# Backward dV and dK stored, and V loaded, a whole head at a time

## The chip, the cores and the metric

One core of a Trainium2 chip runs the kernel once. The metric is the device time of one execution in microseconds (us); shorter is better. Times of single executions of the kernel before are 1365.99, 1366.36 and 1366.83 us, median 1366.36 us.

## The reference, cut to what matters

One token with 640 features goes through an adaptively normalised attention block with a cache of 32 heads (8192 positions, 192 features each) and through a small mixer and MLP; then all gradients for the inputs are computed from `grad_out`.

```python
mod = (silu(c) @ w_mod).reshape(1, 6, 1, -1)      # sa, ca, ga, sb, cb, gb
h = layernorm(x) * (1 + ca) + sa
q = (h @ wq)                                       # 32 heads x 192
p = softmax(einsum('bhqd,bhkd->bhqk', q, k_cache) * 192 ** -0.5)
o = einsum('bhqk,bhkd->bhqd', p, v_cache)
x = x + ga * (o @ wo)
h = layernorm(x) * (1 + cb) + sb
x = x + gb * B(h)                                  # w1, w2, w3, w4 and gelu
# results: out, and d/d(x, k_cache, v_cache, wq, wo, w3, w4, c, w_mod)
```

With one query, the gradient of the cache is an outer product for each head: dV = p (8192) x do (192), and dK = dS (8192) x q (192), where dS = p * (V @ do - c). So K and V are read, V a second time in the backward pass, and dK and dV are written. Each of these has 32 heads of 3072 KB in bf16 (3.146 MB).

## The kernel before, in words

The positions of a head lie on 128 partitions, 64 positions each, so one head is 24576 contiguous bytes per partition both in DRAM and in SBUF. A half (t = 0 or 1) is 32 positions, 12288 bytes per partition, 1536 KB.

**Buffers.** `k_mem` (six halves) holds K in the forward pass. In the backward pass its halves 0 to 4 receive dV and dK, and half 5 is slot 4 of V. `v_mem` (four halves) holds V: slots 0 to 3. Slot 5 is a tile of the pool `bv`.

**Backward pass.** Iteration i of 32 (the loop near the end, over `HS`) treats head h = 31 - i and prepares the next head `nxt`:
- `bwd_mult(h, t)` (L133 through `mul`, matmuls L1109): VectorE (DVE) multiplies a half of V in place by do; TensorE (PE) adds up the product. From i = 20 on this is done one iteration ahead, between `bwd_ds` and `bwd_dk`.
- `bwd_dv(nxt, t)`: dV for the next head. In each half ScalarE (ACT) makes 20 of the 32 positions (L1114) and DVE 12 (L1090); the store of the half follows (L1117).
- `bwd_ds(h)` (L1135 and one more): dS from the sums of PE.
- `bwd_dk(h, t)`: DVE makes a half of dK (L1090) and stores it (L1144).

**Order.** All these loads and stores are issued by one queue, SP's, in program order; an issue that must wait holds all that are behind it. `pin_order` fixes the order on PE, DVE and ACT to the order in the program. `big_tile` hands out the halves of `k_mem` in the order of `big_order`: `[2, 3, 4, 0, 1]` over and over, so a half is written again five halves later.

**Ring.** V halves, blocks of Wo (batches for do) and blocks of Wq and Wmod share one ring of six slots; `ring_load` issues the next load as soon as the content six places earlier has been used (`freed`).

**Side work.** `dwo`, `dw4`, `dw3` stores go along in iterations 1 to 25. The five blocks of Wq (i = 11 to 15) and of Wmod (i = 18 to 22) are multiplied in place (`job_side_mul`), summed on PE, and their gradient blocks are written from the pool `sideout` (`job_side_out`). From i = 24 (`I_SIDE`) three more halves x, y, z (pool `xt`) join the places for dV and dK, and at the very end the four V slots do too (`tail_list`).

Of the kernel before, what the change touches and what calls it, by code (L numbers as in the profile page):

```python
# [20 lines left out]
def kernel(  # L21
# [26 lines left out]
    nc = tc.nc  # L48
# [174 lines left out]

    big = ctx.enter_context(tc.tile_pool(name="big", bufs=1))
    big_order = []
    tail_tiles = {}

    def big_tile(name):
        k = big_order.pop(0)
        if isinstance(k, str):  # L230
            pool, tag = tail_tiles[k]
            if tag[0] == "v":
                return v_tile(pool, int(tag[1:]))
            return pool.tile([P, JH, DH], BF16, name=name, tag=tag)
        return big_half(k)

    k_mem = big.tile([P, 6 * JH, DH], BF16, name="k_mem")

    def big_half(k):
        return k_mem[:, k * JH : (k + 1) * JH, :]  # L240
# [100 lines left out]
    def v_tile(pool, slot):  # L341
        if slot == 4:
            return big_half(5)
        if slot < 4:
            return v_mem[:, slot * JH : (slot + 1) * JH, :]
        return pool.tile([P, JH, DH], BF16, name="V_sb", tag=f"v{slot}")

    def load_v(pool, h, t, slot, eng=None):
        tl = v_tile(pool, slot)
        (eng or nc.sync).dma_start(out=tl, in_=V_hd[h][:, t * JH : (t + 1) * JH, :])  # L350
        return tl
# [434 lines left out]
    BATCHES = [(2, 3, 4), (5, 6, 7), (8, 9, 10), (11, 12, 13), (14, 15)]  # L786
    Q_AT, M_AT = 11, 18
    SIDE_W = {"wq": A_wq, "wm": w_mod}
    ring = []
    for i in range(1, HQ):  # L790
        if i > 1:
            ring += [("v", HS[i], t) for t in range(2)]
        if i % 2 == 1 and 0 < i // 2 < len(BATCHES):
            ring.append(("w", i // 2, 0))
        for name, at in (("wq", Q_AT), ("wm", M_AT)):
            if at <= i < at + NDC:
                ring.append((name, i - at, 0))
    ring_n, freed = [0], set()
    ldq = nc.sync
    NR = 6  # L800

    def ring_slot(n):
        return (4, 5, 2, 3, 0, 1)[n % NR]

    def ring_load():
        while ring_n[0] < len(ring) and (ring_n[0] < 2 or ring_key(ring_n[0] - NR) in freed):
            n = ring_n[0]
            kind, k, t = ring[n]
            slot = ring_slot(n)
            pool = bv if slot > 3 else fv  # L810
            ring_n[0] += 1
            if kind == "v":
                V_b.setdefault(k, {})[t] = load_v(pool, k, t, slot, ldq if n >= 2 else nc.sync)
            elif kind == "w":
                load_wo(k, v_tile(pool, slot))
            else:
                load_side(kind, k, v_tile(pool, slot))

    def load_wo(k, tl):
        lo, n = PS[BATCHES[k][-1]], len(BATCHES[k])  # L820
        tl = tl.rearrange("p j d -> p (j d)")[:, 0 : 3 * n * D].rearrange("p (c r) -> p c r", r=D)
        wo_b[k] = tl
        nc.sync.dma_start(out=tl.rearrange("p (b c) r -> p b (c r)", c=3), in_=A_wo[3 * lo * P : 3 * (lo + n) * P, :].rearrange("(b p c) r -> p b (c r)", p=P, c=3))

    def ring_key(n):
        return ring[n] if n >= 0 else (("v", HS[0], 0), ("v", HS[0], 1), ("v", HS[1], 0), ("v", HS[1], 1))[n]

    ring_load()
    big_order[:] = [0, 4, 1, 4, 1, 2, 3, 4, 1, 2, 3, 4, 0, 1] + [2, 3, 4, 0, 1] * HQ
    st2 = nc.sync  # L830

    do_pb = {}
# [263 lines left out]
    def vec_of(d, h):  # L1096
        return d[h // 2][:, (h % 2) * DH : (h % 2 + 1) * DH]
# [18 lines left out]
    def bwd_dv_store(o, h, t, r0, r1):  # L1116
        st2.dma_start(out=dV_hd[h][:, t * JH + r0 : t * JH + r1, :], in_=o[:, r0:r1, :])  # L1117

    def bwd_dv_dve(o, h, t, na=NAV // 2, ends=(JH,)):
        j0 = t * JH  # L1120
        r0 = 0
        for r1 in ends:
            ra = max(r0, na)
            pairs_outer(o[:, ra:r1, :], bst[h]["P2h"][:, j0 + ra : j0 + r1, :], vec_of(do_pb, h), r1 - ra)
            bwd_dv_store(o, h, t, r0, r1)
            r0 = r1

    def bwd_dv(h, t):
        o = big_tile("dV")
        bwd_dv_act(o, h, t)  # L1130
        bwd_dv_dve(o, h, t)

    def bwd_ds(h):
        dP = bsm.tile([P, J], FP32, name="dP")
# [3 lines left out]
        bst[h]["dS2"] = dS2  # L1138

    def bwd_dk(h, t):  # L1140
        o = big_tile("dK")
        j0 = t * JH
        pairs_outer(o, bst[h]["dS2"][:, j0 : j0 + JH, :], vec_of(q_pb, h), JH)
        st2.dma_start(out=dK_hd[h][:, j0 : j0 + JH, :], in_=o)  # L1144

    def job_mid():
        h2 = ccol(NDC, "h2")
# [33 lines left out]
    side_cm = []  # L1181
    I_SIDE = 24

    def tail_list(seven):
        n = 4 * (HQ - 1 - I_SIDE) - 2
        order = []
        cyc = list(seven)
        for c in range(n):
            if c == n - 10:
                cyc += ["v0", "v1"]  # L1190
                cyc = cyc[-2:] + cyc[:-2]
            if c == n - 6:
                cyc += ["v2", "v3"]
                cyc = cyc[-2:] + cyc[:-2]
            k = cyc.pop(0)
            order.append(k)
            cyc.append(k)
        return order

    dha_c = ccol(NDC, "dha_c")  # L1200
    dsc_c = ccol(NDC, "dsc_c")

# [9 lines left out]
        bcast_cols(col_bf, lo, n, side["bc"][:, lo * P : (lo + n) * P], act_copy)  # L1212

    def job_side_mul(name, u):
        w = side.pop((name, u))
        n = w.shape[1]
        mul(w, w, side["bc"][:, 0:n])
        m = 512 if n % 512 == 0 else 480
        ps = bank("b", name="js_ps")[:, 0:m]
        for k in range(n // m):  # L1220
            nc.tensor.matmul(ps, lhsT=ident_bf, rhs=w[:, k * m : (k + 1) * m], start=(k == 0), stop=(k == n // m - 1))  # L1221
        side["ps"] = ps
        freed.add((name, u, 0))

    def job_side_out(name, u, acc, rows_f, dram):
        nc.vector.reduce_sum(out=acc[:, u : u + 1], in_=side["ps"], axis=AX.X)
        n = dram.shape[1]
        o = side["out"].tile([P, n], BF16, name=name + "_o", tag="wout")
        nc.vector.tensor_scalar(out=o, in0=side["bc"][:, 0:n], scalar1=rows_f[:, u : u + 1], scalar2=None, op0=ALU.mult)
        st2.dma_start(out=dram[u * P : (u + 1) * P, :], in_=o)  # L1230

# [45 lines left out]
    def hook(i):  # L1277
        if i == 0:
            for u in wo_first:
                bwd_ttr(*u)  # L1280
            fin_do(PS[1], 1)
            bwd_dob(PS[1])
            cps[i] = (PS[1], 1, fin_c(PS[1], 1))
            return
        if i % 2 == 1:
            b = (i - 1) // 2
            bwd_wo_mult(b)
            if b > 0:
                freed.add(("w", b, 0))
                ring_load()  # L1290
        if i in fins:
            b = fins[i]
            lo, n = PS[BATCHES[b][-1]], len(BATCHES[b])
            bwd_wo_red(b)
            fin_do_rows(lo, n)
            if i % 2 == 0:
                bwd_dob(HS[i + 2] // 2)
            cps[i] = (lo, n, fin_c(lo, n))
            dq[i] = (lo, n, fin_dq_mm(lo, n))
        if i == 3:  # L1300
            dq[i] = (PS[1], 2, fin_dq_mm(PS[1], 2))
# [8 lines left out]
    o0 = tw.tile([P, JH, DH], BF16, name="dV", tag="w3T_t")  # L1310
    bwd_dv_dve(o0, HS[0], 0, 0, (8, 16, JH))
    h2_mm()
    bwd_dv_dve(big_tile("dV"), HS[0], 1, 0, (JQ, JH))
    bwd_pf(HS[1])
    o1 = big_tile("dV")
    bwd_dv_act(o1, HS[1], 0, 0, JQ)
    q_pb[PS[0]] = pair_bc(bsm, q_bf, PS[0], "q_pb", bank("s", 2, "t_ps", SB[0]))
    bwd_dv_store(o1, HS[1], 0, 0, JQ)
# [19 lines left out]
    for i in range(HQ):  # L1338
# [5 lines left out]
        if i <= AHEAD:  # L1344
            if i in SPLIT:
                bwd_pf(nxt)
            for t in range(2):
                bwd_mult(h, t, 2 if i == 0 else 1)
                if i == t == 0:
                    ring_load()  # L1350
                    c_first = fin_c(PS[0], 1)
                if i in SPLIT:
                    bwd_dv(nxt, t)
        if i not in EARLY:
            ring_load()
        if i - 1 in dq:
            fin_dq(*dq.pop(i - 1))
        if i == 0:
# [4 lines left out]
            for t in range(0 if i > 0 else 1, 2):  # L1363
                bwd_dv(nxt, t)
        if i in EARLY:
            ring_load()
        if i == 0:
            bwd_ds(h)
            dq_last(h)
# [21 lines left out]
        if i == NPH - 1:  # L1391
            fin_dq(*dq.pop(i))
            mm_cm.__exit__(None, None, None)
            psum_cm.__exit__(None, None, None)
            psum[0] = ctx.enter_context(tc.tile_pool(name="psum_s", bufs=1, space=bass.MemoryType.PSUM, reuse_waits="tile"))
            SB[0] = 1024
            for nm, b in (("out", 2), ("bcp", 1)):
                side_cm.append(tc.tile_pool(name="side" + nm, bufs=b, side="right", reuse_waits="tile"))
                side[nm] = side_cm[-1].__enter__()
        for f in J2[i]:  # L1400
            f()
        if i == I_SIDE:
            while side_cm:
                side_cm.pop().__exit__(None, None, None)
            xt = ctx.enter_context(tc.tile_pool(name="xt", bufs=1, side="right", reuse_waits="tile"))
            for k in "xyz":
                tail_tiles[k] = (xt, "xt" + k)
            for n in range(len(ring) - NR, len(ring)):
                slot = ring_slot(n)
                tail_tiles[f"v{n - len(ring) + NR}"] = (bv if slot > 3 else fv, f"v{slot}")  # L1410
            big_order[:] = tail_list(big_order[0:5] + ["x", "y", "z"])
    pin_order(first_ins)


# [28 lines left out]
```

## Time and profile before

| what | before |
|---|---|
| median of three runs | 1366.36 us |
| the profiled execution | 1367.3 us |
| its span, first to last instruction | 1365.5 us |
| moved by DMA queue q1 (the loads and stores above) | 565.86 MB |
| busy share: DVE, ACT, PE | 79%, 67%, 65% |

How to read the views: the page cuts the span into 40 slices and gives a busy digit for each engine and for the 16 DMA engines. A table by stretches gives the busy time of each engine, the granted TensorE clock, the DMA share (the time of all packets over 16 engines' time; packets that overlap on one engine count twice, so it can pass 1) and GB/s. The DMA view of a stretch counts the packets, says how many were under 512 bytes, under 2 KB and under 8 KB, and gives packets, MB and share of each queue; q8 and q14 fetch instructions. The groups of instructions give count, then busy time and mean ns of one, then the idle time of the engine just before them and what ended it. "us to landing" of a DMA counts from its issue to its completion.

### The profile page before, as it was taken

To read this page: it belongs to the slowest core of one execution; us is meant where nothing else is said; L and a number is where in the kernel's file an instruction comes from. 1 tells how busy PE (TensorE), PEld (TensorE's weight loads), DVE (VectorE), ACT (ScalarE), POOL (GpSimd) and SP (SyncE) were. 2 spreads that over 40 slices of the span, in tenths; PEclk is the share of its full clock that TensorE was granted. 3 is DMA by queue.
4 is the path that set the end of the run, shared out by engine and by line. 5 is a ranking of instruction groups with operands and counts; after the bars stand their busy time and mean duration, and the time that the engine had idled before them with its cause. 6 is when DMAs were issued, how large, how long until landed. Compare 5 with 4: busy or idle time off the path is not lost.

```text
span 1365.5 us, 27762 instructions
## 1 busy us (share of the span) xinstructions
PE 886.4 (65%) x11404; PEld 630.7 (46%) x11404; DVE 1080.0 (79%) x1220; ACT 919.9 (67%) x2564; POOL 3.2 (0%) x10
## 2 busy tenths in 40 slices
PE   3799999999999999747756764533334444224440
PEld 3577777777777777736645642211111111011110
DVE  3487888888888887799987778967768778669991
ACT  1387787877888876876776669545567654647770
POOL 0000000000000000000000000000000000000000
PEclk9999999999999999576676666676656766656675
DMA  9999999999999999699999999999999999999997
GB/s 392 417 422 428 425 420 421 420 422 420 424 415 418 424 422 405 259 399 424 423 420 425 427 426 428 424 425 427 426 425 428 426 426 429 424 427 430 427 431 327
DMA packets 55883, 567.64 MB, mean 416 GB/s; under 512 B 5708, under 2 KB 8012, under 8 KB 20172
## 3 DMA queue, kind: packets, MB, share of 16 engines
q1 hardware_dynamic: 55726, 565.86, 98.8%
q8 instruction: 89, 1.46, 0.4%
q14 instruction: 38, 0.31, 0.1%
q10 hardware_dynamic: 30, 0.00, 0.0%
HBM read 339.94 MB, written 225.91 MB: 414 GB/s over the span
## 4 chain that ended last, share of the span: by engine, by line
DMA 49%; PE 22%; DVE 18%; ACT 5%; SPq 2%; issue 2%; DVEq 0%; ACTq 0%
DMA out_dram<-k_mem 29%; DMA v_mem<-in_A_v_cache_dram 17%; PE ps_a L462 7%; DVE k_mem L1090 7%; PE ps_b L473 4%; ACT k_mem L1114 3%; DVE v_mem L133 3%; DMA k_mem<-in_A_k_cache_dram 3%; PE S_ps L402 2%; PE dP_ps L1109 2%; PE kb_ps L479 2%; DVE k_mem L133 1%; SPq L248 1%; DVE prod L133 1%; DVE dP L1135 1%
## 5 line engine op out<-in xcount | busy, mean ns | idle before, releaser
L1114 ACT ACTIVATE k_mem<-do_pb,PF 128x192 bf16<-128x192 bf16 x1126 | 394.2, 440 | 165.1 <-DMA out_dram<-k_mem 164.7
L437 ACT ACTIVATE EK<-k_mem,E_f 128x192 bf16<-128x192 bf16 x992 | 354.5, 442 | 35.8 <-issue 17.7
L1109 PEld LDWEIGHTS <-ident_bf 128*128 128x128 bf16 x1056 | 120.7, 120 | 328.8 <-DVE v_mem L133 114.0
L1109 PE MATMUL dP_ps<-v_mem,ident_bf 128*128 128x512 bf16 (+2 forms) x744 | 168.1, 400 | 139.3 <-DVE v_mem L133 139.3
L133 DVE TENSOR_TENSOR prod<-k_mem,q_pb 128x6144 bf16<-128x6144 bf16 x62 | 207.6, 3349 | 5.2 <-DMA k_mem<-in_A_k_cache_dram 3.9
L1090 DVE TENSOR_TENSOR k_mem<-dS,q_pb 128x6144 bf16<-128x6144 bf16 x59 | 195.9, 3354 | 10.7 <-DMA out_dram<-k_mem 10.1
L462 PE MATMUL ps_a<-EK,v_mem 128*128 128x193 bf16 x1984 | 192.3, 249 | 13.8 <-DMA v_mem<-in_A_v_cache_dram 13.8
L462 PEld LDWEIGHTS <-v_mem 128*128 128x128 bf16 x1984 | 164.3, 98 | 32.2 <-DMA v_mem<-in_A_v_cache_dram 17.3
L1090 DVE TENSOR_TENSOR k_mem<-P2h,do_pb 128x2304 bf16<-128x2304 bf16 (+2 forms) x58 | 78.5, 1360 | 101.4 <-DMA out_dram<-k_mem 100.4
L133 DVE TENSOR_TENSOR v_mem<-v_mem,do_pb 128x6144 bf16<-128x6144 bf16 (+1 forms) x47 | 149.7, 3214 | 0.0
L444 DVE TENSOR_TENSOR EK<-k_mem,P2h 128x1536 bf16<-128x1536 bf16 x124 | 117.8, 950 | 0.2 <-issue 0.2
L473 PE MATMUL ps_b<-EK,v_mem 128*64 128x193 bf16 x1984 | 107.8, 251 | 0.0
L402 PE MATMUL S_ps<-prod,ident_bf 64*64 64x256 bf16 x2976 | 95.8, 275 | 6.4 <-DVE prod L133 6.3
L402 PEld LDWEIGHTS <-ident_bf 64*64 64x64 bf16 x3072 | 85.4, 110 | 26.1 <-issue 23.5
L473 PEld LDWEIGHTS <-v_mem 128*64 128x64 bf16 x1984 | 80.7, 109 | 19.3 <-issue 15.6
L1109 PE MATMUL dP_ps<-k_mem,ident_bf 128*128 128x256 bf16 (+1 forms) x168 | 39.2, 404 | 47.1 <-DVE k_mem L133 47.1
L479 PE MATMUL kb_ps<-EK,hot_bf 128*32 128x384 bf16 x992 | 63.6, 333 | 0.0
L1221 PEld LDWEIGHTS <-ident_bf 128*128 128x128 bf16 x100 | 13.0, 130 | 104.8 <-issue 101.9
L1109 PE MATMUL dP_ps<-V_sb,ident_bf 128*128 128x256 bf16 (+1 forms) x144 | 34.0, 405 | 26.8 <-DVE V_sb L133 26.8
L442 DVE CAST EK<-E_f 128x16 bf16<-128x16 f32 x124 | 24.4, 196 | 32.5 <-ACT EK L437 21.7
L423 ACT ACTIVATE E_f<-sm_ps,negm 128x64 f32<-128x64 f32 x31 | 9.7, 314 | 58.9 <-DVE negm L421 58.9
L406 DVE TENSOR_REDUCE S<-S_ps 128x128 f32<-128x1024 f32 x32 | 39.2, 1224 | 10.8 <-PE S_ps L402 10.7
(289 smaller groups left out, 931.9 us busy)
## 6 DMA issues: line engine op xcount, KB each, us to landing
out_dram<-k_mem SPq DMA_DIRECT2D x114, 1536.0 KB, 23.6
v_mem<-in_A_v_cache_dram SPq DMA_DIRECT2D x55, 1536.0 KB, 21.6
v_mem<-in_A_v_cache_dram SPq DMA_DIRECT2D x25, 3072.0 KB, 17.8
k_mem<-in_A_k_cache_dram SPq DMA_DIRECT2D x20, 3072.0 KB, 14.2
k_mem<-in_A_k_cache_dram SPq DMA_DIRECT2D x24, 1536.0 KB, 19.2
k_mem<-in_A_v_cache_dram SPq DMA_DIRECT2D x10, 1536.0 KB, 20.7
V_sb<-in_A_v_cache_dram SPq DMA_DIRECT2D x9, 1536.0 KB, 23.1
wq<-in_A_wq_dram SPq DMA_DIRECT2D x3, 2560.0 KB, 33.9
```

Source lines behind the costliest of these rows:

```text
L133: nc.vector.tensor_tensor(out=out, in0=a, in1=b, op=ALU.mult)
L402: nc.tensor.matmul(st["S_ps"][c0 : c0 + 64, r, t * JH : (t + 1) * JH, :], lhsT=ident_bf[64 * r : 64 * r + 64, 64 * r : 64 * r + 64], rhs=p ...
L406: nc.vector.reduce_sum(out=st["S2"], in_=st["S_ps"], axis=AX.X)
L437: nc.scalar.activation(out=st["EK"][q][:, jj, 0:DH], in_=K_st[h, t][:, r * JQ + jj, :], func=ACT.Copy, scale=st["E_f"][:, j : j + 1])
L442: nc.vector.tensor_copy(out=EK[:, :, DH : DH + 1], in_=st["E_f"][:, q * JQ : (q + 1) * JQ, None])
L444: nc.vector.tensor_tensor(out=EK[:, NA:JQ, 0:DH].rearrange("p j (d r) -> p j d r", r=2), in0=K_st[h, t][:, r * JQ + NA : (r + 1) * JQ, :]. ...
L462: nc.tensor.matmul(st["A_ps"][:, 0:n], lhsT=V_sb[:, r * JQ + jj, a0:a1], rhs=EK[:, jj, 0:n], start=(q == 0 and jj == 0), stop=(q == 3 and ...
L473: nc.tensor.matmul(st["B_ps"][g : g + 64, 0:n], lhsT=V_sb[:, r * JQ + jj, b0:b1], rhs=EK[:, jj, 0:n], start=(q == 0 and jj < 2), stop=(q = ...
L479: nc.tensor.matmul(kb_ps[g : g + 32, 0 : 2 * DH], lhsT=hot_bf[:, HQ - 1 - h : 2 * HQ - 1 - h], rhs=EK[:, jj : jj + 2, 0:DH], start=(h == 0 ...
L1090: nc.vector.tensor_tensor(out=o.rearrange("p j (d r) -> p j d r", r=2), in0=pairs[:, :, None, :].to_broadcast([P, n, NP2, 2]), in1=vec.rea ...
L1109: nc.tensor.matmul(bst[h]["dP_ps"][:, t * JH + r : t * JH + r + n, :], lhsT=ident_bf, rhs=V_sb[:, :, k * w : (k + 1) * w], start=(k == 0), ...
L1114: nc.scalar.activation(out=o[:, jj, :], in_=vec_of(do_pb, h), func=ACT.Copy, scale=bst[h]["PF"][:, t * JH + jj : t * JH + jj + 1])
```

## The change

Heads are counted here by their place in the backward pass, 0 (h = 31) to 31 (h = 0).

- dV of the heads 9 to 31 and dK of the heads 8 to 30 go to whole places A, B, C of `k_mem` (halves 0-1, 2-3, 4-5), in the order B, C, A. Both halves are computed as before, and one DMA stores the head after the second half. From dV of head 26 on (iteration 25) a fourth place X joins; the last dV and the last dK but one use the two halves of `v_mem` (V1, V0), and the last dK is stored as two halves from (0, 1). Earlier heads use pairs of halves and are stored by halves, in the order of before.
- V of the heads 10 to 31 is loaded by one DMA into one of two whole slots of `v_mem`, issued as soon as both halves of the head two before have been used. Until then there are five V slots (0 to 4).
- Wo blocks, each in turn, go to slot 5 alone. Wq and Wmod blocks use slot 5 and two new tiles of a pool `sidew`; the gradient block is written into the tile of its own block and stored from it, and the block three later is loaded into that tile two iterations after (`W_AT`). The pool `sideout` and the tiles x, y, z are gone.

```diff
-    ring = []
-    for i in range(1, HQ):
-        if i > 1:
-            ring += [("v", HS[i], t) for t in range(2)]
...
+    V_SLOTS = [(2, 3), (0, 1), (4, 2), (3, 0), (1, 4), (2, 3), (0, 1)]
+    v_jobs = [(3 + k, t, sl[t], 1) for k, sl in enumerate(V_SLOTS) for t in range(2)]
+    v_jobs += [(k, 0, 2 * (k % 2 == 0), 2) for k in range(3 + len(V_SLOTS), HQ)]
+    v_occ = dict(enumerate([(1, 0), (1, 1), (0, 0), (0, 1), (2, 0)]))
+    W_USE = [("wq", u, Q_AT + u) for u in range(NDC)] + [("wm", u, M_AT + u) for u in range(NDC)]
+    W_AT = {}
+    for n, (name, u, use) in enumerate(W_USE):
+        W_AT.setdefault(10 + (n > 1) if n < 3 else W_USE[n - 3][2] + 2, []).append(n)
...
+    def ring_load(i):
+        if i == 2:
+            load_wo(1, v_tile(bv, 5))
+        while v_jobs and all(("v", HS[v_occ[sl][0]], v_occ[sl][1]) in freed for sl in range(v_jobs[0][2], v_jobs[0][2] + v_jobs[0][3])):
+            k, t, slot, n = v_jobs.pop(0)
+            for r in range(n):
+                v_occ[slot + r] = (k, t + r)
+            if n == 1:
+                V_b.setdefault(HS[k], {})[t] = load_v(fv, HS[k], t, slot)
             else:
-                load_side(kind, k, v_tile(pool, slot))
+                V_b[HS[k]] = {r: v_tile(fv, slot + r) for r in range(2)}
+                nc.sync.dma_start(out=v_pair(k), in_=V_hd[HS[k]])
+        for n in W_AT.get(i, ()):
+            name, u, use = W_USE[n]
+            load_side(name, u, v_tile(bv, 5) if n % 3 == 0 else side["w"].tile([P, JH, DH], BF16, name="W_sb", tag=f"sw{n % 3}"))
+
+    def out_place(k):
+        if isinstance(k, tuple):
+            return [big_half(x) for x in k], None
+        tl = places[k]
+        return [tl[:, 0:JH, :], tl[:, JH : 2 * JH, :]], tl
+
+    for n, k in enumerate("ABC"):
+        places[k] = k_mem[:, 2 * n * JH : 2 * (n + 1) * JH, :]
...
-    big_order[:] = [0, 4, 1, 4, 1, 2, 3, 4, 1, 2, 3, 4, 0, 1] + [2, 3, 4, 0, 1] * HQ
+    V_b[HS[2]] = {0: load_v(bv, HS[2], 0, 4), 1: load_v(bv, HS[2], 1, 5)}
+    big_order[:] = [0, 4]
+    outs = [(1, 2), (3, 4), (1, 2), (3, 4), (0, 1), (2, 3), (4, 0), (1, 2), (3, 4), (0, 1), (2, 3), (4, 0), (1, 2), (3, 4), (0, 1)]
+    outs += list("BCA") * 11 + ["B"]
+    outs += ["X", "C", "A", "B"] * 2 + ["X", "C", "V1", "V0", (0, 1)]
...
     def bwd_dv(h, t):
-        o = big_tile("dV")
-        bwd_dv_act(o, h, t)
-        bwd_dv_dve(o, h, t)
+        if "dv" not in bst[h]:
+            bst[h]["dv"] = out_place(outs.pop(0))
+        halves, whole = bst[h]["dv"]
+        bwd_dv_act(halves[t], h, t)
+        bwd_dv_dve(halves[t], h, t, store=whole is None)
+        if whole is not None and t == 1:
+            st2.dma_start(out=dV_hd[h], in_=whole)
...
     def bwd_dk(h, t):
-        o = big_tile("dK")
+        if t == 0:
+            bst[h]["dk"] = out_place(outs.pop(0))
+        halves, whole = bst[h]["dk"]
         j0 = t * JH
-        pairs_outer(o, bst[h]["dS2"][:, j0 : j0 + JH, :], vec_of(q_pb, h), JH)
-        st2.dma_start(out=dK_hd[h][:, j0 : j0 + JH, :], in_=o)
+        pairs_outer(halves[t], bst[h]["dS2"][:, j0 : j0 + JH, :], vec_of(q_pb, h), JH)
+        if whole is None:
+            st2.dma_start(out=dK_hd[h][:, j0 : j0 + JH, :], in_=halves[t])
+        elif t == 1:
+            st2.dma_start(out=dK_hd[h], in_=whole)
...
     def job_side_out(name, u, acc, rows_f, dram):
...
-        o = side["out"].tile([P, n], BF16, name=name + "_o", tag="wout")
+        o = side.pop((name, u))
...
-            for nm, b in (("out", 2), ("bcp", 1)):
+            for nm, b in (("w", 1), ("bcp", 1)):
...
+            places["X"] = xt.tile([P, 2 * JH, DH], BF16, name="xt")
+            for k in range(2):
+                places[f"V{k}"] = v_mem[:, 2 * k * JH : 2 * (k + 1) * JH, :]
```

More of the change, by code (lines that the diff above doesn't have):

```diff
@@ L225 @@
     big_order = []
-    tail_tiles = {}
+    places = {}
     def big_tile(name):
[L229 to L235, printed above, removed]
+        return big_half(big_order.pop(0))
     k_mem = big.tile([P, 6 * JH, DH], BF16, name="k_mem")
@@ L788 @@
     SIDE_W = {"wq": A_wq, "wm": w_mod}
-    ring = []
-    for i in range(1, HQ):
-        if i > 1:
-            ring += [("v", HS[i], t) for t in range(2)]
[L793 to L815, printed above, removed]
-            else:
-                load_side(kind, k, v_tile(pool, slot))
+    freed = set()
@@ new lines, with v_pair @@
+    w_half = {}
+    def v_pair(k):
+        return v_mem[:, 2 * (k % 2 == 0) * JH : 2 * (k % 2 == 0) * JH + 2 * JH, :]
+    def ring_load(i):
[7 more added lines that the diff above has]
+                V_b.setdefault(HS[k], {})[t] = load_v(fv, HS[k], t, slot)
+            else:
+                V_b[HS[k]] = {r: v_tile(fv, slot + r) for r in range(2)}
[3 more added lines that the diff above has]
+            load_side(name, u, v_tile(bv, 5) if n % 3 == 0 else side["w"].tile([P, JH, DH], BF16, name="W_sb", tag=f"sw{n % 3}"))
@@ L823, in load_wo @@
         nc.sync.dma_start(out=tl.rearrange("p (b c) r -> p b (c r)", c=3), in_=A_wo[3 * lo * P : 3 * (lo + n) * P, :].rearrange("(b p c) r -> p b (c r)", p=P, c=3))
-    def ring_key(n):
-        return ring[n] if n >= 0 else (("v", HS[0], 0), ("v", HS[0], 1), ("v", HS[1], 0), ("v", HS[1], 1))[n]
-    ring_load()
-    big_order[:] = [0, 4, 1, 4, 1, 2, 3, 4, 1, 2, 3, 4, 0, 1] + [2, 3, 4, 0, 1] * HQ
+    V_b[HS[2]] = {0: load_v(bv, HS[2], 0, 4), 1: load_v(bv, HS[2], 1, 5)}
[3 more added lines that the diff above has]
+    outs += ["X", "C", "A", "B"] * 2 + ["X", "C", "V1", "V0", (0, 1)]
     st2 = nc.sync
@@ L1117, in bwd_dv_store, with bwd_dv_dve @@
         st2.dma_start(out=dV_hd[h][:, t * JH + r0 : t * JH + r1, :], in_=o[:, r0:r1, :])
-    def bwd_dv_dve(o, h, t, na=NAV // 2, ends=(JH,)):
+    def bwd_dv_dve(o, h, t, na=NAV // 2, ends=(JH,), store=True):
         j0 = t * JH
@@ L1124, in bwd_dv_dve @@
             pairs_outer(o[:, ra:r1, :], bst[h]["P2h"][:, j0 + ra : j0 + r1, :], vec_of(do_pb, h), r1 - ra)
-            bwd_dv_store(o, h, t, r0, r1)
+            if store:
+                bwd_dv_store(o, h, t, r0, r1)
             r0 = r1
     def bwd_dv(h, t):
-        o = big_tile("dV")
-        bwd_dv_act(o, h, t)
-        bwd_dv_dve(o, h, t)
+        if "dv" not in bst[h]:
[5 more added lines that the diff above has]
+            st2.dma_start(out=dV_hd[h], in_=whole)
     def bwd_ds(h):
@@ L1182 @@
     I_SIDE = 24
[L1184 to L1198, printed above, removed]
     dha_c = ccol(NDC, "dha_c")
@@ L1214, in job_side_mul @@
     def job_side_mul(name, u):
-        w = side.pop((name, u))
+        w = side[name, u]
         n = w.shape[1]
@@ L1222, in job_side_mul @@
         side["ps"] = ps
-        freed.add((name, u, 0))
     def job_side_out(name, u, acc, rows_f, dram):
@@ L1287, in hook @@
             bwd_wo_mult(b)
-            if b > 0:
-                freed.add(("w", b, 0))
-                ring_load()
+            if 0 < b < len(BATCHES) - 1:
+                load_wo(b + 1, v_tile(bv, 5))
         if i in fins:
@@ L1312 @@
     h2_mm()
-    bwd_dv_dve(big_tile("dV"), HS[0], 1, 0, (JQ, JH))
+    bwd_dv_dve(big_half(big_order.pop(0)), HS[0], 1, 0, (JQ, JH))
     bwd_pf(HS[1])
-    o1 = big_tile("dV")
+    bst[HS[1]]["dv"] = out_place((1, 4))
+    o1 = bst[HS[1]]["dv"][0][0]
     bwd_dv_act(o1, HS[1], 0, 0, JQ)
@@ L1349 @@
                 if i == t == 0:
-                    ring_load()
+                    ring_load(0)
                     c_first = fin_c(PS[0], 1)
@@ L1354 @@
         if i not in EARLY:
-            ring_load()
+            ring_load(i)
         if i - 1 in dq:
@@ L1365 @@
         if i in EARLY:
-            ring_load()
+            ring_load(i)
         if i == 0:
@@ L1405 @@
             xt = ctx.enter_context(tc.tile_pool(name="xt", bufs=1, side="right", reuse_waits="tile"))
[L1406 to L1411, printed above, removed]
+            places["X"] = xt.tile([P, 2 * JH, DH], BF16, name="xt")
+            for k in range(2):
+                places[f"V{k}"] = v_mem[:, 2 * k * JH : 2 * (k + 1) * JH, :]
     pin_order(first_ins)
```

## The prediction

> **What bounds the kernel now.** I read the page's slices first, then the table by stretches, then the DMA view of single stretches.
>
> ```profile
> span 1365.5 us, 27762 instructions
> ...
> DMA  9999999999999999699999999999999999999997
> ...
> q1 hardware_dynamic: 55726, 565.86, 98.8%
> ```
>
> ```profile
> 100.00:480.00 380.00, 364.68 (x6729) 288.92 (x6729) 317.58 (x490) 303.66 (x887) 0.00 (x0) 1.00 1.00 422
> 640.00:860.00 220.00, 138.29 (x802) 105.78 (x801) 184.04 (x177) 154.75 (x409) 0.00 (x0) 0.66 1.01 425
> 860.00:1140.00 280.00, 114.15 (x401) 45.57 (x399) 215.74 (x128) 170.31 (x455) 0.00 (x0) 0.68 1.01 426
> 1160.00:1340.00 180.00, 63.83 (x220) 24.60 (x218) 153.76 (x87) 117.03 (x336) 0.00 (x0) 0.66 1.01 428
> 540.00:580.00 40.00, 31.69 (x493) 29.51 (x491) 31.16 (x89) 30.31 (x78) 2.09 (x2) 0.54 0.73 281
> 1340.00:1365.50 25.50, 0.00 (x0) 0.00 (x0) 0.00 (x0) 0.00 (x0) 0.00 (x0) 0.50 0.69 293
> ```
>
> The last two numbers of a row are the DMA share and GB/s. Outside the middle (540 to 580) and the last 25 us the 16 DMA engines are never short of work, and in the backward pass they move 425 to 428 GB/s. DVE is busy 154 of 180 us in the stretch from 1160, ACT 117: neither is the bound there. What they wait for says the same:
>
> ```profile
> L1114 ACT ACTIVATE k_mem<-do_pb,PF 128x192 bf16<-128x192 bf16 x1126 | 394.2, 440 | 165.1 <-DMA out_dram<-k_mem 164.7
> ...
> L1090 DVE TENSOR_TENSOR k_mem<-P2h,do_pb 128x2304 bf16<-128x2304 bf16 (+2 forms) x58 | 78.5, 1360 | 101.4 <-DMA out_dram<-k_mem 100.4
> ```
>
> ACT stood still for 165 us and DVE for 101 us until a store had left its place. Those waits are the price of a full DMA queue, not its cause. So the change can gain in two ways only: the same bytes pass the DMA engines in less time, or an empty stretch is filled. It can lose by one: the queue runs dry where it is full now. The bytes stay the same, and the two empty stretches lie outside what the change touches (the middle is before the first whole transfer, the end is the drain after the last store is issued).
>
> **The change part by part.** *Fewer and larger packets.* Whole places are handed out 34 times as B, C, A and 12 times by the last list without its pair (0, 1): 46 stores. V is loaded whole for heads 10 to 31: 22 loads. That is 68 transfers of 3072 KB for 136 of 1536 KB. Each has one packet per partition, so each engine moves 8 packets of 24576 bytes for 16 of 12288: 68 x 8 = 544 packets fewer on every engine. What is one packet worth, apart from its bytes? No row shows a store of 24576 bytes; loads of it are in the forward pass.
>
> Four stretches, by their DMA view: 40 to 60 (blocks of wq in 4096-byte packets, and halves), 60 to 80 (halves, forward), 341 to 362 (wholes, forward), 1320 to 1340 (halves, stores):
>
> ```profile
> DMA packets 1309, 8.38 MB, mean 419 GB/s; under 512 B 76, under 2 KB 76, under 8 KB 903
> ...
> q1 hardware_dynamic: 1307, 8.35, 101.5%
> q8 instruction: 2, 0.03, 0.7%
> ```
>
> ```profile
> DMA packets 769, 8.42 MB, mean 421 GB/s; under 512 B 84, under 2 KB 84, under 8 KB 84
> ...
> q1 hardware_dynamic: 764, 8.36, 99.7%
> ```
>
> ```profile
> DMA packets 415, 9.00 MB, mean 428 GB/s; under 512 B 48, under 2 KB 48, under 8 KB 48
> ...
> q1 hardware_dynamic: 412, 8.95, 99.8%
> q8 instruction: 3, 0.05, 1.0%
> ```
>
> ```profile
> DMA packets 786, 8.58 MB, mean 429 GB/s; under 512 B 88, under 2 KB 88, under 8 KB 88
> ...
> q1 hardware_dynamic: 786, 8.58, 100.6%
> ```
>
> The packets under 512 bytes are completions; I leave them in the time and out of the count. A half then takes 99.7% x 320 us / 680 = 469.2 ns in the forward pass and 100.6% x 320 / 698 = 461.2 ns in the stores; a whole takes 99.8% x 336 / 364 = 921.2 ns. In the stretch from 40 there are 827 packets of 4096 bytes and 404 halves: 324.8 us less 404 x 469.2 ns leaves 163.5 ns for 4096 bytes. Three of these carry the bytes of one half and take 490.5 ns, 21.3 more for two packets more: 10.7 ns a packet. Part of that overlaps with the next packet, since the shares pass 100%: by (324.8 + 2.2 - 320) / 1231 = 5.7 ns a packet from 40, by 1.9 us / 698 = 2.8 ns in the stores. I take the mean of the two, 4.2 ns, off: **6.5 ns a packet, 544 x 6.5 = 3.5 us**.
>
> The bounds come from the same rows. Two halves of the forward pass against a whole there: 938.4 - 921.2 = 17 ns for the packet saved, 9.2 us in all. Two halves of the stores against the forward whole: 922.4 - 921.2 = 1.2 ns, 0.7 us. The second compares a stage with instruction fetches (1.0% on q8) with one without, and the first mixes 20 us stretches of unlike neighbours; 6.5 is between, nearer to the lower end, and I keep both for the range. Below zero I see no reason: the 422 GB/s of the forward whole-head stretch (100 to 480) are less than the 425 to 428 of the halves in the backward pass, but it also carries instruction fetches (q8) and the 480 KB pieces of Wo, and the halves of the forward pass (60 to 80) run at 421.
>
> *Coarser places.* A place is now free only when a whole head has landed, and a store starts only when a whole head is made. I follow one iteration of the steady part (i = 10 to 19). The rows:
>
> ```profile
> 1147.86 1.22 DVE L1135 TENSOR_REDUCE dP<-dP_ps 128x64 f32<-128x1024 f32 x1
> ...
> 1149.39 6.62 DVE L133 TENSOR_TENSOR v_mem<-v_mem,do_pb 128x6144 bf16<-128x6144 bf16 x2
> ...
> 1182.98 6.62 DVE L1090 TENSOR_TENSOR k_mem<-dS,q_pb 128x6144 bf16<-128x6144 bf16 x2
> ...
> 1214.71 3.10 PE L1109 MATMUL dP_ps<-V_sb,ident_bf 128*128 128x512 bf16 x12
> ...
> 1222.06 13.92 ACT L1114 ACTIVATE k_mem<-do_pb,PF 128x192 bf16<-128x192 bf16 x40
> ```
>
> ```profile
> out_dram<-k_mem SPq DMA_DIRECT2D x13, 1536.0 KB, 23.2
> v_mem<-in_A_v_cache_dram SPq DMA_DIRECT2D x4, 1536.0 KB, 25.8
> ```
>
> ```profile
> out_dram<-dV SPq DMA_DIRECT2D x2, 384.0 KB, 2.4
> ```
>
> The second fence is the stretch 1200 to 1300: a half needs 3.7 us of DMA and lands 23 to 26 us after its issue, so some 20 us of work lie ahead of it. The third (560 to 620) shows a transfer with nothing ahead: 2.4 us for 0.9 us of bytes, so about 1.5 us to complete. A whole takes 3.146 MB / 429 GB/s = 7.3 us. SP issues in the order V(i+2), dV(i+1), dK(i).
> - dK(i) goes where dV(i) was. Behind dV(i) in the queue lie dK(i-1), V(i+2) and dV(i+1): 22 us. Until dK(i) is issued pass 1.5 + 6.6 us. **14 us of work remain.**
> - dV(i+1) goes where dK(i-2) was. Behind that lie V(i+1), dV(i), dK(i-1), V(i+2): 29 us; needed are 1.5 + 13.9 (ACT; the two parts of DVE beside it). 14 us remain.
> - V(i+2) needs V(i) used up: DVE makes dK(i-1) once dV(i-1) has landed, then multiplies, then PE ends: 1.5 + 6.6 + 6.6 + 3.1 = 17.8 us. Behind dV(i-1) lie dK(i-2), V(i+1), dV(i), dK(i-1): 29 us. 11 us remain.
>
> So the reserve falls from about 20 to 11 to 14 us and does not end. In front of the whole store SP can hold the load behind it, but these sums have that order already. From i = 20 the multiplication is done an iteration ahead and the reserve of V grows.
>
> *Wq and Wmod.* Same ten loads and ten stores. A block loaded in iteration U+2 waits on SP for the store of iteration U, which has a whole iteration behind it (with a block of Wq 3 x 7.3 + 2 x 3.7 = 29 us); the multiplication comes one iteration later. Nothing waits long: 0, and hidden by the reserve if it does. *Wo, first block of the ring*: it is issued in iteration 2, at the place where the row of SP below stands, and needed where DVE's row stands; a load of that stretch (620 to 700) lands after 15.1 us.
>
> ```profile
> 623.98 0.55 SPq L350 DMA_DIRECT2D k_mem<-in_A_v_cache_dram  x1
> ```
>
> ```profile
> 644.33 3.08 DVE v_mem L133
> ```
>
> ```profile
> v_mem<-in_A_v_cache_dram SPq DMA_DIRECT2D x4, 1536.0 KB, 15.1
> ```
>
> That is 5 us to spare, and a late landing would be borne by the queue: 0. *Places and sums otherwise* (X, V1, V0; six halves for five): 0, since the DMA engines are full either way.
>
> **Sum.** The profiled execution took 1367.3 us: span 1365.5 and 1.8 around it; it is 0.9 above the median. 1367.3 - 3.5 = 1363.8 for it, and 1366.36 - 3.5 = **1362.9 us** for the median of three. A measurement can tell about 0.2% from no change, 2.7 us: below 1363.6 it is faster, above 1369.1 slower.
>
> **The rivals.**
> *The packet costs less than I take.* Against my 6.5 ns stand the 1.2 ns of the stores' half and the equal GB/s of the forward stretches with halves (421) and wholes (422). At 3.5 ns the gain is 544 x 3.5 = 1.9 us: 1364.5, within 0.2%. A change that does not do what it says ends here too: were whole stores cut into halves by the DMA, V alone would gain 22 x 8 x 6.5 ns = 1.1 us: 1365.2. The Trainium skill ("DMA: Bandwidth & Descriptors", section "Why small descriptors are slow (HBM only)") speaks for this rival: besides a cycle for each 32 bytes a packet costs about three fixed cycles, so by its account 3 of 387 for a half. Of 20 us x 16 / 698 = 458.5 ns that would be 3.6 ns, an estimate, and 1364.4 us. The 10.7 ns of the small packets, even less the 4.2 of overlap, speak against it.
> *The reserve runs out.* Where side work delays DVE or ACT by more than the 11 to 14 us, the queue is dry until the whole head is made, where before a half sufficed. Up to there it costs nothing, beyond it each us late is a us lost, in up to 22 iterations. Were each of these 0.4 us short: 8.8 - 3.5 = 5.3 us slower, 1371.7. For it: DVE is busy 85% in the stretch from 1160. Against it: in the forward pass V has the same two whole slots, and the share stays at 1.00.
> *The packet costs all of 17 ns*: 1357.2.
>
> **How the numbers follow.** Forecast 0.53 (5 to 8.7 ns, 1361.6 to 1363.7), cheap packet or no whole stores 0.26, reserve 0.17, dear packet 0.04. All of the reserve's chance but 0.01 is above 1369.1; of the forecast 0.02 falls short of 1363.6. Faster 0.55, same 0.29, slower 0.16. The range leaves out the dear packet and the far half of the reserve: 1360.5 to 1371.
>
> **What would show it.** Right: in stretches of whole transfers the DMA view counts about half the packets, at 430 to 431 GB/s with a share still at 1.00 or above; wholes land after 18 to 25 us; the middle and the drain stay as they are. Wrong: 428 GB/s with full engines (the packet is cheap), or shares under 1.00 in the stretch from i = 9 on, with SP waiting for DVE or ACT ahead of whole stores (the reserve).

## The result and the profile after

The changed kernel took 1362.74 us in the median of 8 runs (1361.67 to 1363.02), the kernel before 1366.4 us (8 runs, 1365.64 to 1367.15): ratio 0.9972, 95% interval 0.9961 to 0.9983. That is 3.7 us less; 3.5 were forecast. The profiled execution took 1362.73 us with a span of 1360.9. The page of the changed kernel, its counts:

```profile
span 1360.9 us, 27631 instructions
...
DMA packets 46090, 567.63 MB, mean 417 GB/s; under 512 B 4620, under 2 KB 6924, under 8 KB 19084
...
q1 hardware_dynamic: 45934, 565.86, 98.7%
...
L1117 ACT ACTIVATE k_mem<-do_pb,PF 128x192 bf16<-128x192 bf16 x1086 | 378.7, 440 | 124.3 <-DMA out_dram<-k_mem 105.0
...
L1093 DVE TENSOR_TENSOR k_mem<-dS,q_pb 128x6144 bf16<-128x6144 bf16 x62 | 205.4, 3353 | 50.4 <-DMA out_dram<-k_mem 50.1
...
L1093 DVE TENSOR_TENSOR k_mem<-P2h,do_pb 128x2304 bf16<-128x2304 bf16 (+2 forms) x56 | 74.4, 1358 | 8.4 <-DMA out_dram<-k_mem 7.6
```

The bytes of q1 are the same to the last digit, the packets 9792 fewer: 68 x (128 packets and 16 completions), so all 68 transfers are whole and none was cut up. The compute engines still wait for stores to leave their places, ACT less (105 us, before 165), and DVE at another point: before dK 50 us, before dV 8 where it was 100.

The table by stretches of the changed kernel (last two numbers: DMA share, GB/s):

```profile
100.00:480.00 380.00, 362.53 (x6712) 287.31 (x6714) 317.07 (x487) 303.23 (x886) 0.00 (x0) 1.00 1.00 421
540.00:580.00 40.00, 31.37 (x494) 29.14 (x495) 31.35 (x90) 30.30 (x78) 2.07 (x2) 0.55 0.75 286
640.00:860.00 220.00, 139.12 (x815) 102.99 (x815) 186.77 (x179) 159.08 (x422) 0.00 (x0) 0.68 1.01 427
860.00:1140.00 280.00, 103.05 (x384) 42.13 (x386) 216.21 (x130) 171.42 (x462) 0.00 (x0) 0.68 1.01 429
1160.00:1336.00 176.00, 62.07 (x212) 23.85 (x212) 135.98 (x76) 108.86 (x314) 0.00 (x0) 0.65 1.01 431
```

The engines are as full as before, but they move 429 and 431 GB/s where it was 426 and 428. The forward pass and the middle did not change. One stretch that holds nothing but whole transfers (1300 to 1320; by their issues and landings two stores, with parts of two loads of V around them), in its DMA view:

```profile
DMA packets 397, 8.63 MB, mean 431 GB/s; under 512 B 46, under 2 KB 46, under 8 KB 46
...
q1 hardware_dynamic: 397, 8.63, 100.4%
```

By the prediction's reckoning a whole takes 100.4% x 320 us / 351 = 915.3 ns, two halves of stores 2 x 461.2 = 922.4: 7.1 ns less for one packet less. The figure is rough, since one packet more or less in the count shifts it by 2.6 ns. Another profile of the changed kernel has, in the same stretch, 47 completions among 399 packets:

```profile
q1 hardware_dynamic: 399, 8.65, 100.5%
```

That is 913.6 ns for a whole, 8.8 less than two halves.

How much a fixed stretch moves can be compared between kernels. From 860 to 1320 the kernel before moved (first fence) and the changed one (second):

```profile
q1 hardware_dynamic: 20041, 196.07, 100.8%
```

```profile
q1 hardware_dynamic: 12391, 197.35, 100.5%
```

1.28 MB more in 460 us; at 429 GB/s that is 3.0 us of the 3.7. The rest of the whole transfers lies before and behind this stretch. (The other profile of the changed kernel moved 197.32 MB here; two profiles of one kernel can differ by 0.2.)

### The profile page after: what moved, and what is told of

It reads as the page before. It is cut to its first block, busy times and chain, and to the rows that moved or that the text cites. A ratio compares the mean times of both kernels' runs of the same rounds, so it can differ in the third digit from the quotient of the medians.

```text
span 1360.9 us, 27631 instructions
## 1 busy us (share of the span) xinstructions
PE 870.3 (64%) x11401; PEld 621.5 (46%) x11404; DVE 1079.7 (79%) x1220; ACT 918.1 (67%) x2564; POOL 3.2 (0%) x10
## 4 chain that ended last, share of the span: by engine, by line
DMA 45%; PE 18%; DVE 15%; ACT 6%; issue 2%; DVEq 0%; SPq 0%; ACTq 0%
DMA out_dram<-k_mem 24%; DMA v_mem<-in_A_v_cache_dram 17%; DVE k_mem L1093 7%; PE ps_a L456 6%; ACT k_mem L1117 6%; PE ps_b L467 3%; DVE v_mem L133 2%; PE dP_ps L1112 2%; DMA W_sb<-in_w_mod_dram 2%; PE S_ps L396 2%; PE kb_ps L473 1%; DMA k_mem<-in_A_k_cache_dram 1%; DVE prod L133 1%; DVE k_mem L133 1%; PE t_ps L741 0%
## 5 line engine op out<-in xcount | busy, mean ns | idle before, releaser
L1117 ACT ACTIVATE k_mem<-do_pb,PF 128x192 bf16<-128x192 bf16 x1086 | 378.7, 440 | 124.3 <-DMA out_dram<-k_mem 105.0
L1112 PE MATMUL dP_ps<-v_mem,ident_bf 128*128 128x512 bf16 (+2 forms) x960 | 217.5, 400 | 259.6 <-DVE v_mem L133 259.6
L1093 DVE TENSOR_TENSOR k_mem<-dS,q_pb 128x6144 bf16<-128x6144 bf16 x62 | 205.4, 3353 | 50.4 <-DMA out_dram<-k_mem 50.1
L133 DVE TENSOR_TENSOR v_mem<-v_mem,do_pb 128x6144 bf16<-128x6144 bf16 (+1 forms) x62 | 199.1, 3248 | 32.9 <-DMA v_mem<-in_A_v_cache_dram 32.9
L1093 DVE TENSOR_TENSOR k_mem<-P2h,do_pb 128x2304 bf16<-128x2304 bf16 (+2 forms) x56 | 74.4, 1358 | 8.4 <-DMA out_dram<-k_mem 7.6
L196 ACT CAST do_pb<-bc_ps 128x384 bf16<-128x384 f32 x15 | 7.1, 471 | 92.7 <-PE bc_ps L192 92.7
L1117 ACT ACTIVATE xt<-do_pb,PF 128x192 bf16<-128x192 bf16 x120 | 41.8, 439 | 0.1
```

Source lines behind the costliest of these rows:

```text
L133: nc.vector.tensor_tensor(out=out, in0=a, in1=b, op=ALU.mult)
L1093: nc.vector.tensor_tensor(out=o.rearrange("p j (d r) -> p j d r", r=2), in0=pairs[:, :, None, :].to_broadcast([P, n, NP2, 2]), in1=vec.rea ...
L1112: nc.tensor.matmul(bst[h]["dP_ps"][:, t * JH + r : t * JH + r + n, :], lhsT=ident_bf, rhs=V_sb[:, :, k * w : (k + 1) * w], start=(k == 0), ...
L1117: nc.scalar.activation(out=o[:, jj, :], in_=vec_of(do_pb, h), func=ACT.Copy, scale=bst[h]["PF"][:, t * JH + jj : t * JH + jj + 1])
```

## The experiments

Two theories to begin with. *Size* (the expectations call it the packet theory): an engine pays for each packet besides its bytes, and 544 packets fewer are the gain. *Places*: the gain comes from six halves in place of five, and from tiles of their own for Wq and Wmod. A third, *transfer*, splits the first: the cost belongs to a DMA (its issue, its completions), not to its packets.

**Two and four pieces.**

```diff
-            st2.dma_start(out=dV_hd[h], in_=whole)
+            for r in range(2):            # 4 in the second run; dK and V likewise
+                w = 2 * JH // 2
+                st2.dma_start(out=dV_hd[h][:, r * w : (r + 1) * w, :], in_=whole[:, r * w : (r + 1) * w, :])
```

Two pieces. Expected: 

> The changed kernel with its places, waits and order kept, but each of the 68 whole transfers issued as two of half a head, one right behind the other, when the whole head is ready. Packet theory (each packet costs its engine about 6.4 ns besides its bytes): 544 packets per engine come back, +3.5 us on 1362.7, about 1366.2 us; stretches of these transfers at 427 to 429 GB/s again. Place theory (the gain came from six halves instead of five and from the new tiles for Wq and Wmod, not from the size): stays at 1362.7.

Measured: 1366.46 us (11 runs, 1365.57 to 1367.3), ratio 1.0 (0.9991 to 1.0008). All of the gain is gone with places, waits and order unchanged. The theory of places falls. From 860 to 1320 it moved:

```profile
q1 hardware_dynamic: 20054, 196.20, 100.8%
```

as little as the kernel before. Four pieces. Expected: 

> As the run with two pieces, but four transfers of a quarter head (6144 bytes per partition) for each of the 68. Packet theory with the same cost for every size: 3 x 544 = 1632 packets more per engine, +10.4 us: 1373.1. If the cost fell away with deeper queues or were hidden between neighbours: less than 1370. Place theory: 1362.7.

Measured: 1375.8 us (1375.02 to 1376.52), ratio 1.0068 (1.0054 to 1.0082). That is 9.3 us more than two pieces for 1088 packets more per engine, 8.6 ns each, against 3.7 / 544 = 6.8 ns for the first doubling. Its page counts 75310 packets on q1, and the same stretch moved less with engines as full as ever:

```profile
q1 hardware_dynamic: 34875, 192.95, 101.4%
```

**Packet or transfer, stores.** A place whose halves don't touch needs two packets per partition in one DMA. (The edit, cut: the halves and the stores take the same shape, and the places are handed out in the order C, A, B.)

```diff
-        places[k] = k_mem[:, 2 * n * JH : 2 * (n + 1) * JH, :]
+        places[k] = k_mem.rearrange("p (t k j) d -> p t k (j d)", t=2, k=3)[:, :, n, :]
```

Expected: 

> Places A, B, C made of halves that are not neighbours (0 and 3, 1 and 4, 2 and 5), each head still stored by one DMA: 41 stores keep their single issue and their 16 completions but have two packets of 12288 bytes per partition (V, X and the two places in V's memory as in the changed kernel). Packet theory: 41 x 8 = 328 packets more per engine, +2.1 us: 1364.8. Transfer theory (the cost belongs to a DMA's issue and completion): 1362.7. Place theory: 1362.7.

Measured: 1523.48 us, ratio 1.1145 (1.1129 to 1.116). Neither theory had that. Page and table by stretches of this run:

```profile
q1 hardware_dynamic: 51182, 565.86, 90.7%
...
L1095 DVE TENSOR_TENSOR k_mem<-dS,q_pb 128x6144 bf16<-128x6144 bf16 x62 | 205.9, 3354 | 190.9 <-DMA out_dram<-k_mem 190.5
```

```profile
860.00:1140.00 280.00, 88.00 (x315) 35.86 (x318) 166.63 (x99) 134.05 (x358) 0.00 (x0) 0.63 0.82 325
```

The packets are those planned (41 x 128 more), but the queue is dry: DVE stood 190 us before dK until a store had landed, against 50. The places interleave (0 and 3, 1 and 4, 2 and 5), so each spans bytes of the two others, and the waits came out as if they overlapped. The next run has the same packets without that (cut):

```diff
+    HB, GAP = JH * DH, 16        # 32 bytes; k_flat: k_mem with 4 * GAP more
+        lo = n * (2 * HB + GAP)
+        places[k] = k_flat[:, lo : lo + 2 * (HB + GAP)].rearrange("p (t x) -> p t x", t=2)[:, :, 0:HB]
```

(Four one-column constants share a tile to make room.) Expected: 

> As the run with places of halves that are not neighbours, but the two halves of each of A, B and C lie beside each other with 32 bytes between them, so that no place overlaps another: 41 stores keep one issue and 16 completions each and have two packets of 12288 bytes per partition. Packet theory (6.8 ns a packet, by the run with two pieces): 41 x 8 = 328 packets more per engine, +2.2 us: 1364.9. Transfer theory (the cost belongs to a DMA's issue and completions): 1362.7. And the 1523 us of the run before came from the waits between overlapping places, not from the packets: no stretch below 425 GB/s here.

Measured: 1364.44 us (11 runs, 1363.56 to 1365.58), ratio 0.9982 (0.9973 to 0.9991), with the same 51182 packets. So the 160 us were waits. The step over the changed kernel, 1.7 us, is near the spread, so both were run side by side. Expected: 

> The changed kernel once more, beside the two runs that follow on the same chip, since their differences are near the spread of a median. All theories: 1362.7, give or take 0.5.

and 

> The places with 32 bytes between their halves once more. Packet theory: 1.7 to 2.2 us above the changed kernel of this call. Transfer theory: equal to it.

Measured: the changed kernel 1362.61 us (1361.42 to 1363.6), ratio 0.997 (0.9958 to 0.9981); the gap 1364.05 (1363.42 to 1365.44), ratio 0.9983 (0.9974 to 0.9991). 1.4 us, after 1.7: 4.4 to 5.2 ns for each of 328 packets. So for stores the second packet costs, without a second transfer. One rival was not tested: the 32 bytes also shift where the halves begin in SBUF, and no run has the shift without the second packet.

**Packet or transfer, loads of V.**

```diff
-                nc.sync.dma_start(out=v_pair(k), in_=V_hd[HS[k]])
+                for r in range(2):
+                    w = 2 * JH // 2
+                    nc.sync.dma_start(out=v_pair(k)[:, r * w : (r + 1) * w, :], in_=V_hd[HS[k]][:, r * w : (r + 1) * w, :])
```

Expected: 

> The changed kernel with only the 22 loads of V in two pieces each, the 46 stores whole. Packet theory: 22 x 8 = 176 packets more per engine, +1.2 us: 1363.9. If only stores gain from the size: 1362.7; if only loads do: 1366.4.

Measured: 1364.8 us (11 runs, 1364.15 to 1366.21), ratio 0.9985 (0.9976 to 0.9994): 2.1 us for 176 packets. Again beside the changed kernel, expected: 

> V in two pieces once more. Packet theory with 6.8 ns for loads and stores alike: 1.2 us above the changed kernel of this call; if packets of loads cost more, as the first run seemed to say (11.9 ns), 2.1 us.

Measured: 1364.56 us (1363.56 to 1365.75), ratio 0.9983 (0.9974 to 0.9992): 2.0 us, 11 ns for each packet. Then one transfer with two packets per partition, by a gap of 32 bytes between the halves of V's two whole slots. Expected: 

> The changed kernel, but the two halves of each whole slot of V have 32 bytes between them: the 22 loads of V keep one issue each and have two packets of 12288 bytes per partition (176 packets more per engine), all else whole. Two pieces per load cost 2.0 us (11.4 ns a packet), more than the stores' 4.4 to 5.2 ns. If a load's packet costs that: 1364.6. If the packet costs 5 to 7 ns as elsewhere and the rest belongs to the second transfer: 1363.5 to 1363.9. If all belongs to the transfer: 1362.7.

Measured: 1362.19 us (5 runs, 1361.57 to 1362.74), ratio 0.996 (0.9947 to 0.9974). The same packets in one transfer cost nothing that can be seen. (This run is from another chip. It lies 4.3 us under the kernel before there; the changed kernel lay 4.2 under it beside the second run with two pieces.) So with V the loss comes with the second transfer, not with the second packet. From 860 to 1320 moved the two runs with two pieces (first and second fence) and the one with the gap (third):

```profile
q1 hardware_dynamic: 14974, 197.27, 100.6%
```

```profile
q1 hardware_dynamic: 14966, 197.07, 100.5%
```

```profile
q1 hardware_dynamic: 14689, 197.23, 100.7%
```

Against the changed kernel's 197.35 MB that is 0.2, 0.7 and 0.3 us, and the first two are profiles of one kernel. So most of the 2.0 us of the two pieces is not in the mean rate of this stretch. It shows at the end. The DMA view from 1350 to 1370 gives GB/s in slices of 0.5 us; the changed kernel (first) and the first run with two pieces (second):

```profile
GB/s 467 393 442 369 418 418 418 123 172 123 74 74 74 49 49 49 25 25 0 0 0 0 0 0 0 0 0 0 0 0 0 0 0 0 0 0 0 0 0 0
```

```profile
GB/s 467 393 418 467 221 221 147 172 74 74 74 123 49 25 25 25 25 25 25 25 25 25 0 0 0 16 0 0 0 16 0 0 0 0 0 0 0 0 0 0
```

The changed kernel moves its last data at 1359, this one at 1361. In its last nine slices 25 GB/s flow, about what one of 16 engines moves (430 / 16 = 27). So one engine is left with some 4 us of work when the others are done, though up to 1320 the kernels had moved nearly the same. Why that engine is late stays open.

**The forward pass by halves.**

```diff
-    K_WHOLE = range(5, 25)
+    K_WHOLE = range(0)
...
-    V_WHOLE = HQ - 4
+    V_WHOLE = 3
```

Expected: 

> The changed kernel with the 20 whole loads of K and 25 of V in the forward pass loaded by halves instead. Packet theory, if loads in the forward pass cost the same: 45 x 8 = 360 packets more per engine x 6.8 ns = +2.4 us: 1365.1. If the forward pass gains nothing from the size, as its equal GB/s with halves and wholes seemed to say: 1362.7.

Measured: 1365.59 us (11 runs, 1364.73 to 1367.36), ratio 0.9993 (0.9985 to 1.0002): 2.9 us above the changed kernel. The stretch 100 to 480, where 44 of the 45 loads lie, doesn't show it. The changed kernel (first) and this one:

```profile
q1 hardware_dynamic: 9408, 159.13, 99.4%
```

```profile
q1 hardware_dynamic: 15796, 159.16, 99.9%
```

The same megabytes in the same time: in the rate, neither the second packet nor the second transfer of these loads costs anything. The loss stands later, where the forward pass ends. The changed kernel (first) and this one from 520 to 540:

```profile
520.00:540.00 20.00, 19.57 (x394) 16.06 (x392) 15.64 (x32) 14.16 (x40) 0.00 (x0) 0.97 1.02 402
```

```profile
520.00:540.00 20.00, 18.35 (x351) 14.90 (x349) 14.52 (x26) 14.19 (x40) 0.00 (x0) 1.00 0.93 361
```

The share falls from 1.02 to 0.93: the queue runs dry for a while, and 0.8 MB less is moved, 1.9 us of the 2.9. So the 2.9 us are not a price of 360 packets. That halves leave less work ahead in the queue there is the likely reason; no run tests it.

**The reserve.** All dV in B, all dK in C:

```diff
-    outs += list("BCA") * 11 + ["B"]
+    outs += list("BC") * 17
```

Expected: 

> The changed kernel with two whole places instead of three up to the head of iteration 24: all dV in B, all dK in C. Reserve theory: dV of the next head must wait until dV of this one has landed; behind that lie only dK and V, 14.7 us, and 15.4 us pass until it is issued, so the queue is dry for 0.7 us or more in each of some 16 iterations, and the longer the later it gets its turn: 10 to 60 us slower than the changed kernel, 1373 to 1423, shares under 1.00 from iteration 9 on. If the queue doesn't need the third place: 1362.7.

Measured: 1373.92 us (1372.88 to 1376.97), ratio 1.0059 (1.0044 to 1.0075): 11.2 us slower than the changed kernel, at the low end of what was expected. Its table by stretches:

```profile
860.00:1140.00 280.00, 114.51 (x406) 45.86 (x408) 215.95 (x127) 168.87 (x455) 0.00 (x0) 0.67 1.00 421
1140.00:1320.00 180.00, 59.00 (x215) 23.23 (x215) 145.11 (x86) 116.80 (x336) 0.00 (x0) 0.65 0.99 418
```

429 and 430 GB/s have become 421 and 418, with shares of 1.00 and 0.99 where they were 1.01: the queue runs dry now and then. From 860 to 1320 this run moved

```profile
q1 hardware_dynamic: 12194, 192.91, 99.5%
```

4.4 MB less than the changed kernel, 10 us of the 11.2. This is how the rival would have looked.

**The dry spot at the end.** Just before the last dK but one is stored (1338) the changed kernel's engines are short of work:

```profile
1335.00:1339.00 4.00, 0.00 (x0) 0.00 (x0) 4.00 (x2) 0.00 (x0) 0.00 (x0) 0.80 0.74 320
...
1350.00:1355.00 5.00, 0.00 (x0) 0.00 (x0) 0.00 (x0) 0.00 (x0) 0.00 (x0) 0.50 0.79 334
```

```diff
-        return [tl[:, 0:JH, :], tl[:, JH : 2 * JH, :]], tl
+        return [tl[:, 0:JH, :], tl[:, JH : 2 * JH, :]], None if k == "V0" else tl
```

Expected: 

> The changed kernel, but the last dK but one (its place is V0) is stored by halves, the first 3.3 us earlier. In the changed kernel the DMA engines are short of work for about 1.2 us around 1335 to 1339, just ahead of that store. If that is its lateness: 1361.5, and the share stays at 1.00 there. If the engines lose that time at the end anyway (the slowest engine decides): 1362.7.

Measured: 1362.56 us (1361.29 to 1362.93), ratio 0.997 (0.9959 to 0.9982): no faster. The spot was filled:

```profile
1335.00:1339.00 4.00, 0.00 (x0) 0.00 (x0) 3.96 (x3) 0.00 (x0) 0.00 (x0) 0.73 0.95 406
...
1350.00:1355.00 5.00, 0.00 (x0) 0.00 (x0) 0.00 (x0) 0.00 (x0) 0.00 (x0) 0.50 0.49 209
1355.00:1360.50 5.50, 0.00 (x0) 0.00 (x0) 0.00 (x0) 0.00 (x0) 0.00 (x0) 0.50 0.12 51
```

What was moved earlier is missing later: the mean rate falls off from 1350 instead of 1355, and the end stays. The last 20 us of this run (1350 to 1370) in slices of 0.5 us:

```profile
GB/s 393 270 246 197 172 147 172 147 197 147 147 98 98 74 49 49 49 0 0 0 0 0 0 0 0 0 0 0 0 0 0 0 0 0 0 0 0 0 0 0
```

The rate falls in steps to that of two engines, and the last data move at 1358.5, in the changed kernel at 1359. So some engines finish up to 8 us before the last, and filling idle time of the others doesn't help it. That the last one was not dry before is concluded from this, not seen: the view gives the sum of the 16.

## Why the prediction was right, point by point

- *The DMA engines are the bound, and their empty stretches stay.* Right: shares of 1.00 to 1.01, 286 GB/s in the middle where it was 281. The dry spot at 1335 was not foreseen; filling it gained nothing.
- *544 packets fewer per engine.* Right: 9792 on q1 less the completions are 8704, 544 on each of 16.
- *6.5 ns a packet, 3.5 us.* Right as a sum: 3.7 us / 544 = 6.8 ns by the time. The step behind it was too simple. It gave stores and loads one price, paid by the packet. The runs split the 3.7 us. The stores' part is 1366.46 - 1364.56 = 1.9 us for 368 packets, 5.2 ns each; this is a difference of two runs, since none cuts the stores alone. V's part is 2.0 us for 176 packets, 11 ns each, and it is no packet's price: it comes with the second transfer and shows mostly in the last engine's end. At 6.5 ns the stores would have given 2.4 us and V 1.1. The two errors nearly cancel, and that is luck. So is some of the 6.5 itself: it was made from loads of 4096 bytes, less the mean of two overlaps.
- *The bounds, 1.2 and 17 ns.* Both were read from loads or from two unlike stages. The low one set halves of stores against a whole of the forward pass; against the stretch of whole transfers, mostly stores, the difference is 7.1 to 8.8 ns. The high one came from forward loads, where halves cost nothing in the rate from 100 to 480.
- *Coarser places, 11 to 14 us of reserve left.* The sign was right: no stretch went dry until 1335. The size was too low. The changed kernel from 1000 to 1100 (A, B, C alone) and from 1200 to 1300 (with X):

```profile
out_dram<-k_mem SPq DMA_DIRECT2D x8, 3072.0 KB, 27.4
```

```profile
out_dram<-k_mem SPq DMA_DIRECT2D x7, 3072.0 KB, 31.5
v_mem<-in_A_v_cache_dram SPq DMA_DIRECT2D x5, 3072.0 KB, 30.4
```

  A whole store lands 27 us after its issue in the steady part and 31 later; 18 to 25 had been expected. Less 7.3 us for itself and 1.5 to complete, that is 19 to 22 us of other work ahead. The sums counted V, dV and dK alone and left out the side work in the same queue; whether this is the whole difference stays open. The two-places run then came to 0.7 us x 16 = 11 us as the same sums gave at least, and 11.2 were measured. As the sums were 5 us or more too low for three places, a hit that close is in part luck; the order (three places hold, two don't) is what was shown.
- *Wq, Wmod, Wo and the places otherwise: 0.* With two pieces the time is the one before (1366.46 against 1366.63 on the same chip), so these together come to nothing measurable.
- *The rival of the cheap packet, 1.9 us.* Wrong for the whole: 3.7 us were gained. The rule of the Trainium skill ("DMA: Bandwidth & Descriptors", section "Why small descriptors are slow (HBM only)"), about three fixed cycles a packet, was 3.6 ns by the prediction's estimate; the runs show more for stores, 4.4 to 5.2 ns for the second packet. For loads the rival was nearer than the forecast: the equal GB/s of the forward stretches was good evidence, since 44 loads by halves cost nothing in the rate, and V's second packet in one transfer cost nothing either.

## What to carry to other kernels

When the DMA queue is full all the time, count packets and transfers per engine, not bytes alone: here some 5 ns for each packet of 12288 bytes that the stores saved, 1 part in 90, while loads showed no price in the rate. Before making transfers larger, follow for each place what lies in the queue between its landing and the next issue from it, since a coarser place pays only while that stays above the time to fill it. And a full queue is a matter of the slowest engine: idle time that a mean share shows near the end may cost nothing, and a loss may not show in it.

## What the runs showed of the hardware that was not expected

- A second transfer can cost more than a second packet: V in two transfers 1364.56 and 1364.8 us, in one transfer with two packets 1362.19. For stores the packet is the larger part (1.4 to 1.7 us, for 41 of 46 stores, of about 1.9, the last being 1366.46 less 1364.56).
- The 16 DMA engines end far apart, and the last one sets the time: with V in two pieces one engine's rate (25 GB/s) flows for the last 4 us.
- About eight transfers are in flight at most, whatever their size. Four pieces, 1240 to 1320, and SP's waits in the same run from 860 to 1340:

```profile
out_dram<-k_mem SPq DMA_DIRECT2D x24, 768.0 KB, 15.0
```

```profile
SPq L1163 <- DMA v_mem<-in_A_v_cache_dram: 90.5, 60, 2.2
SPq L810 <- DMA out_dram<-k_mem: 87.6, 59, 1.9
```

  15.0 us at 1.8 us each are 8.2 transfers, and SP waits for landings of other tensors each time. In the kernel before, 23 to 27 us at 3.7 are 6 to 8. So halving the size halves the work that can lie ahead (15 us), and whole heads reach 30 us with four. That a limit on their number makes SP wait is argued from these rows, not shown by itself. It need not be the chip's: the trace counts the landings on eight semaphores, with nearly equal numbers on each (566 to 592 in the changed kernel), so the program itself may let only eight run at a time.
